# An instruction planner with a readiness slack, a shorter landing margin, early multiply-adds on GpSimd, and row loads cut nine to eight

## The chip, the cores and the metric

The kernel runs on one core of a Trainium2 chip. The time is device microseconds (us) of one execution. A kernel is given by the median of several executions, and two kernels are compared by ratios, which are explained at the result.

## The reference

Two strided convolutions with gelu, a projection, a joint tensor `tanh(fe + ge)` and an output projection; the kernel computes the output and the seven gradients of it.

```python
B, T, D, K, U = 2, 16000, 256, 3, 8           # all bf16
def _fwd_reference(x, w1, w2, g, w_f, w_g, w_o):
    # h = gelu(conv3(x, w1))[:, ::2]           T -> T/2
    # f = gelu(conv3(h, w2))[:, ::2]           T/2 -> T/4 = 4000
    fe = jnp.einsum("btd,de->bte", f, w_f)
    ge = jnp.einsum("bud,de->bue", g, w_g)
    j = jnp.tanh(fe[:, :, None, :] + ge[:, None, :, :])
    return jnp.einsum("btud,dv->btuv", j, w_o)

def reference(x, w1, w2, g, w_f, w_g, w_o, grad_out):
    _out, _vjp = jax.vjp(_fwd_reference, x, w1, w2, g, w_f, w_g, w_o)
    return (_out, *_vjp(grad_out))
```

## The kernel before

The 4,000 output rows of each batch are worked in chunks, 18 in all. The kernel does not write its instructions in a fixed order. Every operation is recorded with the engines that may do it and a modelled cost; a planner then walks through modelled time and hands out the operations. Its key for an operation is the latest start that still meets the modelled end, so a small key is urgent.

```python
class Flow:
    WAKE = {"PE": 45.0, "ACT": 25.0, "DVE": 25.0, "POOL": 280.0, "SP": 60.0}
    MARGIN = 6500.0                              # ns added to a load before its consumers may be placed
    # ...
            for e, lst in avail.items():         # each engine, its operations with all inputs planned
                t, wake, cand = T[e], self.WAKE[e], None
                for o in lst:
                    s = o.ready + wake           # earliest modelled start
                    # ... (DMA lanes, free buffers)
                    k = (max(s, t), o.key, o, e) # first that which can start first, then the urgent one
                    if cand is None or k < cand:
                        cand = k
    # ...
                o.done = ring[e] + 2000.0 + o.margin     # when the planner takes a load to have landed
```

The derivative of gelu is a polynomial on bf16 tiles. Its three one-input steps, here called the multiply-adds, run on VectorE:

```python
    def conv_gelu(W, taps, h_buf, h_ap, g_buf, g_ap, news):
        # ... per half: matmuls -> ps; ScalarE Square -> g_sq, Gelu -> HT or FT; VectorE (g_sq+1)*ps -> g_s
        op("ACT", c_act(N), lambda e: nc.scalar.activation(out=s[:, :, :W], in_=s[:, :, :W], func=ACT.Tanh, scale=c), ...)
        op("DVE", c_dve(N, 0.25), lambda e: nc.vector.tensor_scalar(
            out=sq[:, :, :W], in0=sq[:, :, :W], scalar1=3.0 * c, scalar2=c, op0=ALU.mult, op1=ALU.add), ...)
        op("DVE", c_dve(N, 0.5), lambda e: nc.vector.tensor_tensor(
            out=sq[:, :, :W], in0=sq[:, :, :W], in1=h_ap(None), op=ALU.mult), ...)
        op("DVE", c_dve(N, 0.25), lambda e: nc.vector.tensor_scalar(
            out=sq[:, :, :W], in0=sq[:, :, :W], scalar1=-0.5, scalar2=None, op0=ALU.add), ...)
        op("DVE", c_dve(N, 0.25), lambda e: nc.vector.tensor_scalar(
            out=s[:, :, :W], in0=s[:, :, :W], scalar1=-1.0, scalar2=1.0, op0=ALU.mult, op1=ALU.add), ...)
        op("DVE", c_dve(N, 0.5), lambda e: nc.vector.tensor_tensor(
            out=g_ap(), in0=s[:, :, :W], in1=sq[:, :, :W], op=ALU.mult), ...)
```

Names that the profile uses: FE is the projection of the chunk, copied out of PSUM and transposed by TensorE (`psb<-ident,FE`); JT and JR are the tanh of the joint tensor in two layouts; GWO is the gradient of `w_o`, whose matmuls read JR; OUT and GX are the outputs; X are the rows of `x` for the gradient of `w1`, two overlapping loads of nine rows each for a chunk.

## Time and profile before

| | before |
|---|---|
| median of 3 runs | 807.73 us (807.53 to 807.94) |
| span of the profiled run | 803.7 us |
| columns of all 6,124 matmuls with the small cost of each | about 761 us |
| TensorE / VectorE / ScalarE / GpSimd busy | 97 / 95 / 88 / 11% |

How to read it: three engines are nearly full, so the averages tell little, and the stages must be looked at one by one. The prediction below shows the lines that do so.

### The profile page before, as it was taken

The page shows a single profiled execution, that of the slowest core. Times are in us where ns is not written, and L with a number is a line of the kernel's source. Part 1 is how long each engine was busy: PE and PEld are TensorE (multiplying, and loading weights), DVE is VectorE, ACT ScalarE, POOL GpSimd, SP SyncE. Part 2 cuts the span into 40 slices and gives each one's busy share as a digit, 9 for nine tenths or more (in the row PEclk, how much of TensorE's full clock was granted, in tenths as well). Part 3 has the DMA queues.
Part 4 walks back from the last instruction along what each step waited for, and adds up shares of the span by engine and source line. Part 5 has one row for each costly group of instructions (what it writes and reads, how often), then busy time and mean ns, then how long its engine had stood idle before and what let it go on. Part 6 is the DMA issues. An engine that isn't in the chain of part 4 may idle for free.

```text
span 803.7 us, 16871 instructions
## 1 busy us (share of the span) xinstructions
PE 776.6 (97%) x6124; PEld 574.1 (71%) x6124; DVE 761.3 (95%) x1743; ACT 705.9 (88%) x1138; POOL 87.6 (11%) x256
## 2 busy tenths in 40 slices
PE   8799999999999999999999999999999999999996
PEld 6566667676776867787777667676776867788885
DVE  5989999999999999998989999999999999999894
ACT  6999999998898999997889999998898999997482
POOL 1001110200101010010011100000102000011121
PEclk9989999999999999999999999999999999999999
DMA  7999999999999999999999999999999999999995
GB/s 199 221 219 226 242 228 217 240 244 252 209 277 220 248 257 188 251 214 240 219 230 174 259 252 242 245 228 268 208 261 216 254 256 234 241 232 221 212 216 138
DMA packets 403360, 184.81 MB, mean 230 GB/s; under 512 B 326310, under 2 KB 394956, under 8 KB 403276
## 3 DMA queue, kind: packets, MB, share of 16 engines
q1 hardware_dynamic: 400764, 182.53, 102.8%
q10 hardware_dynamic: 2384, 1.18, 0.5%
q8 instruction: 48, 0.79, 0.4%
q14 instruction: 36, 0.29, 0.1%
q0 software_dynamic: 128, 0.03, 0.0%
HBM read 52.48 MB, written 50.34 MB: 128 GB/s over the span
## 4 chain that ended last, share of the span: by engine, by line
PE 48%; DVE 28%; ACT 19%; issue 3%; DMA 1%; SPq 0%; DVEq 0%; ACTq 0%
PE ps L412 40%; PE GWO L412 7%; DVE NGZ L855 5%; ACT JT L788 5%; DVE ZS L863 5%; ACT JSQ L845 4%; DVE g_s L603 3%; DVE JR L801 2%; ACT g_sq L599 2%; ACT JR L808 2%; DVE ACC L912 2%; ACT HT L601 2%; ACT OUT_SB L423 2%; DVE g_sq L614 1%; DVE GH L971 1%
## 5 line engine op out<-in xcount | busy, mean ns | idle before, releaser
L788 ACT ACTIVATE JT<-FE,GE 128x512 bf16<-128x512 bf16 (+2 forms) x288 | 183.1, 676 | 7.9 <-PE ps L412 6.9
L412 PE MATMUL ps<-GOT,WT 128*128 128x512 bf16 (+3 forms) x640 | 152.5, 333 | 2.6 <-DMA GOT<-GO_R 2.2
L412 PE MATMUL ps<-WO,JT 128*128 128x256 bf16 x1024 | 151.7, 272 | 2.1 <-DVE GH L981 1.7
L855 DVE SCALAR_TENSOR_TENSOR NGZ<-JSQ,ps 128x512 f32<-128x512 bf16 (+2 forms) x252 | 151.5, 605 | 0.0
L808 ACT ACTIVATE JR<-JR 128x1024 bf16<-128x1024 bf16 x128 | 136.4, 1071 | 9.3 <-DVE JR L801 9.2
L845 ACT ACTIVATE JSQ<-JT 128x1024 bf16<-128x1024 bf16 (+2 forms) x128 | 126.2, 986 | 15.8 <-DVE NGZ L855 14.7
L412 PE MATMUL GWO<-GO_R,JR 128*128 128x256 bf16 x1024 | 133.2, 274 | 2.0 <-ACT JR L808 2.0
L412 PEld LDWEIGHTS <-JT 128*128 128x128 bf16 x1024 | 99.0, 98 | 49.0 <-issue 4.6
L863 DVE TENSOR_TENSOR ZS<-ZS,NGZ 128x512 f32<-128x512 f32 (+2 forms) x216 | 131.1, 612 | 0.0
L423 ACT CAST OUT_SB<-ps 128x512 bf16<-128x512 f32 x192 | 110.5, 596 | 22.7 <-PE ps L412 22.6
L412 PEld LDWEIGHTS <-JR 128*128 128x128 bf16 x1028 | 99.6, 98 | 24.8 <-ACT JR L808 4.4
L412 PEld LDWEIGHTS <-WT 128*128 128x128 bf16 x1000 | 88.5, 98 | 39.2 <-issue 4.4
L412 PEld LDWEIGHTS <-W 128*128 128x128 bf16 x720 | 65.9, 98 | 55.0 <-issue 2.3
L412 PE MATMUL ps<-WT,GH 128*128 128x256 bf16 x732 | 97.1, 273 | 0.7 <-DVE NGZ L855 0.7
L412 PE MATMUL ps<-XC,W 128*128 128x512 bf16 (+4 forms) x432 | 93.0, 343 | 1.1 <-DMA XC<-in_x_dram 1.1
L412 PE MATMUL ps<-GHR,X 128*128 128x256 bf16 x768 | 90.5, 273 | 0.0
L801 DVE TENSOR_TENSOR JR<-FER,GEB 128x1024 bf16<-128x1024 bf16 x128 | 87.2, 686 | 0.1
L412 PEld LDWEIGHTS <-X 128*128 128x128 bf16 x768 | 74.9, 98 | 9.7
L412 PEld LDWEIGHTS <-GH 128*128 128x128 bf16 x732 | 71.2, 98 | 12.3 <-issue 1.7
L603 DVE SCALAR_TENSOR_TENSOR g_s<-g_sq,ps 128x512 bf16<-128x512 bf16 (+2 forms) x108 | 65.7, 610 | 12.0 <-ACT HT L601 9.0
L912 DVE TENSOR_TENSOR ACC<-ACC,ps 128x512 f32<-128x512 f32 x96 | 64.7, 678 | 8.5 <-PE ps L412 8.2
L599 ACT ACTIVATE g_sq<-ps 128x512 bf16<-128x512 f32 (+2 forms) x108 | 58.5, 545 | 8.4 <-PE ps L412 7.6
(127 smaller groups left out, 1003.4 us busy)
## 6 DMA issues: line engine op xcount, KB each, us to landing
GO_R<-in_grad_out_dram SPq DMA_DIRECT2D x56, 512.0 KB, 5.1
out_dram<-OUT_SB SPq DMA_DIRECT2D x56, 512.0 KB, 4.5
X<-in_x_dram SPq DMA_DIRECT2D x28, 576.0 KB, 6.1
out_dram<-GX_SB SPq DMA_DIRECT2D x28, 512.0 KB, 6.1
GO_R<-in_grad_out_dram SPq DMA_DIRECT2D x8, 256.0 KB, 5.2
out_dram<-OUT_SB SPq DMA_DIRECT2D x8, 256.0 KB, 2.9
GOT<-GO_R SPq DMA_TRANSPOSE x72, 6.5
out_dram<-w_out SPq DMA_DIRECT2D x9, 128.0 KB, 1.9
```

The costliest lines, as they stand in the source:

```text
L412: nc.tensor.matmul(ps_ap, lhsT=lhsT, rhs=rhs, start=start, stop=stop)
L423: nc.scalar.copy(out=dst(), in_=src())
L599: op("ACT", c_act(W, True), lambda e, mt=mt, ps=ps: nc.scalar.activation(out=sq[:, mt, :W], in_=ps[:, :W], func=ACT.Square, scale=GELU_SQR ...
L601: go = op("ACT", c_act(W, True), lambda e, mt=mt, ps=ps: nc.scalar.activation(out=h_ap(mt), in_=ps[:, :W], func=ACT.Gelu_apprx_tanh), r=[p ...
L603: op("DVE", c_dve(W), lambda e, mt=mt, ps=ps: nc.vector.scalar_tensor_tensor(out=s[:, mt, :W], in0=sq[:, mt, :W], scalar=1.0, in1=ps[:, :W ...
L788: op("ACT", c_act(W, ptr=True), lambda e, j=j, mt=mt: nc.scalar.activation(out=JT[:, j, mt, :W], in_=S["FE"][:, mt, :W], func=ACT.Tanh, bi ...
L801: op("DVE", c_dve(n * 2 * D, 0.5), lambda e, lo=lo, n=n, m=m, JR=JR: nc.vector.tensor_tensor(out=JR[:m, lo % 2:lo % 2 + n], in0=S["FER"][: ...
L808: op("ACT", c_act(n * 2 * D), lambda e, lo=lo, n=n, m=m, JR=JR: nc.scalar.activation(out=JR[:m, lo % 2:lo % 2 + n], in_=JR[:m, lo % 2:lo % ...
L845: nc.scalar.activation(out=JSQ[:, :, :W], in_=JT[:, j, :, :W], func=ACT.Square)
L855: op("DVE", c_dve(W) + 6, lambda e, d2=d2, ps=ps, u=u, zap=zap, JSQ=JSQ: nc.vector.scalar_tensor_tensor(out=zap(), in0=JSQ[:, d2, :W], sca ...
L863: op("DVE", c_dve(W), lambda e, d2=d2, dst=dst, NGZ=NGZ: nc.vector.tensor_tensor(out=dst[:, d2, :W], in0=ZS[:, d2, :W], in1=NGZ[:, :W], op ...
L912: op("DVE", c_dve(512), lambda e: nc.vector.tensor_tensor(out=acc_ap().rearrange("p k d -> p (k d)"), in0=acc_ap().rearrange("p k d -> p ( ...
```

## The change

The planner should prefer operations that have been ready for a while (SLACK), so that an engine isn't put right behind its producer and made to stand by a small modelling error. Loads are taken to land 3 us sooner (MARGIN). The multiply-adds of the first three chunks, where VectorE is full, may go to GpSimd, whose cost the planner takes as 130 ns plus 1 ns a column. The second row load takes eight rows, since the ninth was there already.

```diff
-    MARGIN = 6500.0
+    SLACK = {"PE": 500, "ACT": 300, "DVE": 300, "POOL": 0.0, "SP": 0.0}
+    MARGIN = 3500.0
...
-                    k = (max(s, t), o.key, o, e)
+                    k = (max(s + slack, t), o.key, o, e, max(s, t))
...
+        nr = 9 - h
...
-                                             ap=[[4 * nb * D, hi - lo], [1, 9 * D]]),
+                                             ap=[[4 * nb * D, hi - lo], [1, nr * D]]),
...
+        ts = lambda n: (("POOL", "DVE"), (130.0 + n, c_dve(n, 0.25))) if early else ("DVE", c_dve(n, 0.25))
-        op("DVE", c_dve(N, 0.25), lambda e: nc.vector.tensor_scalar(
+        op(*ts(N), lambda e: (nc.gpsimd if e == "POOL" else nc.vector).tensor_scalar(
   (three times; early is g_ < 3)
```

(Cut: the same slack carried through the planner's loop, the row addresses, and the `early` argument in three calls.)

More of the change, by code (lines that the diff above doesn't have):

```diff
@@ L184, in run @@
             for e, lst in avail.items():
-                t, wake, cand = T[e], self.WAKE[e], None
+                t, wake, cand, slack = T[e], self.WAKE[e], None, self.SLACK[e]
                 for o in lst:
@@ L214, in run @@
                 continue
-            s, _, o, e = best
+            _, _, o, e, s = best
             if o.lead:
@@ L529, in load_x9 @@
         for k, (lo, hi) in enumerate(row_parts(r0, P)):
-            dma(LOADQ, lambda lo=lo, hi=hi: X9[:].rearrange("p f d -> p (f d)")[lo:hi],
-                lambda lo=lo, hi=hi: bass.AP(tensor=src.tensor, offset=src.offset + (4 * (c0 + nb * lo) - 3 + 8 * h) * D,
-                                             ap=[[4 * nb * D, hi - lo], [1, 9 * D]]),
-                r=[], w=[(X9, ("m", k))], bytes_=(hi - lo) * 4608, new=new, at=at, hold=hold, cost=550.0)
+            dma(LOADQ, lambda lo=lo, hi=hi: X9[:, 0:nr].rearrange("p f d -> p (f d)")[lo:hi],
+                lambda lo=lo, hi=hi: bass.AP(tensor=src.tensor, offset=src.offset + (4 * (c0 + nb * lo) - 3 + 9 * h) * D,
+                                             ap=[[4 * nb * D, hi - lo], [1, nr * D]]),
+                r=[], w=[(X9, ("m", k))], bytes_=(hi - lo) * 512 * nr, new=new, at=at, hold=hold, cost=550.0)
             new = []
@@ L582, in part, with conv_gelu @@
         return p_
-    def conv_gelu(W, taps, h_buf, h_ap, g_buf, g_ap, news):
+    def conv_gelu(W, taps, h_buf, h_ap, g_buf, g_ap, news, early=False):
         hk = (lambda mt: (h_buf[0], (h_buf[1], mt))) if isinstance(h_buf, tuple) else (lambda mt: (h_buf, mt))
@@ L615, in conv_gelu @@
             out=sq[:, :, :W], in0=sq[:, :, :W], in1=h_ap(None), op=ALU.mult), r=[sq, hk(0), hk(1)], w=[sq], at=late)
-        op("DVE", c_dve(N, 0.25), lambda e: nc.vector.tensor_scalar(
+        op(*ts(N), lambda e: (nc.gpsimd if e == "POOL" else nc.vector).tensor_scalar(
             out=sq[:, :, :W], in0=sq[:, :, :W], scalar1=-0.5, scalar2=None, op0=ALU.add), r=[sq], w=[sq], at=late)
-        op("DVE", c_dve(N, 0.25), lambda e: nc.vector.tensor_scalar(
+        op(*ts(N), lambda e: (nc.gpsimd if e == "POOL" else nc.vector).tensor_scalar(
             out=s[:, :, :W], in0=s[:, :, :W], scalar1=-1.0, scalar2=1.0, op0=ALU.mult, op1=ALU.add),
@@ L684, in stage_a @@
                 for i, c in ((0, 1), (1, 2), (2, 3)) for kt in range(KT)]
-        conv_gelu(W, (taps, S["XCk"] + [W1]), (HT, "o"), both(HTo, P), G1o, lambda: G1o[:, :, P:P + W], [HT, G1o])
+        conv_gelu(W, (taps, S["XCk"] + [W1]), (HT, "o"), both(HTo, P), G1o, lambda: G1o[:, :, P:P + W], [HT, G1o], g_ < 3)
         for nm, T_, k_, keys in (("HTo", HTo, (HT, "os"), [(HT, ("o", 0)), (HT, ("o", 1))]),
@@ L707, in stage_a @@
         taps += [(lambda kt=kt: W1[:, 0, kt], lo, lambda f=f, kt=kt: f(kt)) for lo, f in S["xback"] for kt in range(KT)]
-        conv_gelu(W, (taps, S["XCk"] + [W1, S["XS"]]), (HT, "e"), both(HTe), G1e, lambda: G1e[:, :, 0:W], [G1e])
+        conv_gelu(W, (taps, S["XCk"] + [W1, S["XS"]]), (HT, "e"), both(HTe), G1e, lambda: G1e[:, :, 0:W], [G1e], g_ < 3)
         if Wp > W:
@@ L717, in stage_a @@
                 for i, SRC, lo in ((2, HTo, P), (1, HTe, 0), (0, HTo, r0)) for kt in range(KT)]
-        S["go"] = [conv_gelu(W, (taps, hok + hek + [W2]), FT, both(FT), G2, lambda: G2[:, :, 0:W], [FT, G2])]
+        S["go"] = [conv_gelu(W, (taps, hok + hek + [W2]), FT, both(FT), G2, lambda: G2[:, :, 0:W], [FT, G2], g_ < 3)]
         pad_tail(g_, FT)
@@ L1020, in stage_de @@
             X5 = [load_x9(b, c0, nb_of[g_], h, t0 + dt * 0.2, hold_) for h in range(nb_of[g_] // 2)]
-            xrow = lambda m, bl, f, d2: X5[bl // 2][:m, bl % 2 * 4 + f, d2 * P:(d2 + 1) * P]
+            xrow = lambda m, bl, f, d2: (X5[0][:m, 4 * bl + f, d2 * P:(d2 + 1) * P] if 4 * bl + f < 9 else
+                                         X5[1][:m, 4 * bl + f - 9, d2 * P:(d2 + 1) * P])
         else:
```

## The prediction

> **What bounds the kernel now.** I read the engine totals on the page first, then the groups of TensorE's instructions by form, then the table of windows, TensorE's waits, and the timeline of the worst place.
>
> ```profile
> PE 776.6 (97%) x6124; PEld 574.1 (71%) x6124; DVE 761.3 (95%) x1743; ACT 705.9 (88%) x1138; POOL 87.6 (11%) x256
> PEclk9989999999999999999999999999999999999999
> ```
>
> TensorE is busy 97% of the 803.7 us span, but VectorE (95%) and ScalarE (88%) stand close behind, so the average does not say which one holds the end in a given stage. The clock row has a dip in its third slice. As busy matmuls overlap, I count columns instead: adding count times width over all matmul forms gives 6,124 matmuls with 1,789,040 columns. Back to back, eight 256-column matmuls take 0.87 us in the chain of waits, 0.109 us each, which is 256 columns at 2.4 per ns plus 2.3 ns. So the floor of TensorE is 745.4 us of columns, about 761 us with the small cost per matmul. 803.7 - 761 leaves **about 42 us in which no column streams**. The windows say where:
>
> ```profile
> core 0: us, PE busy (x) PEld busy (x) DVE busy (x) ACT busy (x) POOL busy (x), PEclk, DMA share, GB/s
> 20.00:40.00 20.00, 15.19 (x112) 10.08 (x110) 19.73 (x57) 18.94 (x36) 1.40 (x4) 0.99 1.11 220
> 40.00:45.00 5.00, 3.26 (x19) 2.36 (x20) 5.00 (x15) 4.66 (x6) 0.89 (x2) 0.50 1.04 267
> 45.00:50.00 5.00, 5.00 (x30) 2.91 (x29) 4.00 (x11) 4.77 (x7) 0.00 (x0) 0.86 0.99 241
> 60.00:80.00 20.00, 18.12 (x134) 12.37 (x133) 20.00 (x46) 19.72 (x31) 3.02 (x7) 1.00 1.01 221
> 80.00:100.00 20.00, 19.62 (x137) 12.78 (x135) 20.00 (x43) 20.00 (x33) 2.63 (x6) 1.00 1.09 243
> 100.00:120.00 20.00, 18.45 (x140) 12.87 (x138) 20.00 (x42) 19.92 (x31) 2.14 (x7) 1.00 1.08 226
> 300.00:400.00 100.00, 99.74 (x843) 76.95 (x842) 96.29 (x230) 87.25 (x155) 11.52 (x39) 1.00 1.03 222
> ```
>
> There are two regimes. From 20 to 120 us VectorE and ScalarE are both full and TensorE is not: the elementwise engines bound this stage. From 120 us TensorE is full and they are not. Adding spacings minus columns over the TensorE timeline, I place the 42 us so: about 6 before 20 us (first loads), about 15 from 20 to 120 us, about 14 spread over 120 to 790 us in waits too short to show as idle time, and about 7 after the last matmul at 796.4 us. Only the middle two, 29 us, can be had by this change. The waits that do show:
>
> ```profile
> PE psb L656 <- DVE FE L428: 4.2, 5, 2.0
> PE ps L412 <- DVE NGZ L855: 3.0, 7, 0.6
> PE ps L412 <- DMA GOT<-GO_R: 2.2, 2, 1.2
> PE GWO L412 <- ACT JR L808: 2.0, 3, 1.0
> PE ps L412 <- DVE GH L981: 1.7, 2, 0.9
> ```
>
> The largest is a matmul put right behind its own producer: the transposes of FE wait for the copy of FE out of PSUM. The worst one is at 39 us:
>
> ```profile
> 40.69 1.28 DVE L428 CAST FE<-ps 128x512 bf16<-128x512 f32 x2
> 41.42 0.29 PE L656 MATMUL psb<-ident,FE 128*128 128x128 bf16 x1 [1.95 <-DVE FE L428]
> 43.17 1.91 PE L412 MATMUL GWO<-GO_R,JR 128*128 128x256 bf16 x8
> ```
>
> VectorE runs back to back from 20 us to here, so the copies start 1.3 us after their matmuls are through. TensorE stands, and then the eight matmuls of GWO take 1.91 us where they take 1.03 to 1.05 elsewhere: the clock has been halved (0.50 in the window 40 to 45 us).
>
> [...] a ZS addition beside GpSimd copies took 0.88 us against a median of 0.68. [...] No multiply-add on GpSimd is in this trace; its memsets grow from 540 ns (512 elements) to 1,166 ns (1,280), or 0.82 ns an element, so I estimate about 1.0 us for 1,024.
>
> **The change part by part.** All numbers of instructions come from comparing the instruction orders of the two kernels.
>
> (1) GpSimd for the early multiply-adds. 22 instructions move, 16 of 1,024 columns and 6 of 512. On VectorE they are spaced 0.34 us and about 0.21 us, so 16 x 0.34 + 6 x 0.21 = 6.7 us leave VectorE in the first 85 us, where it is full. [...] a loss of 0.2 to 0.3 us for each of the 22 gives back 4.4 to 6.6 us. Net **-1 us**, and I would not be surprised by zero.
>
> (2) Operations ready for a while first. TensorE's instructions are the same 6,124 in another order. What changes can be read from the order: the matmul time that stands between the FE matmuls and the transposes that need their copy had a median of 1.4 us over the 18 chunks, with 0.87 four times or so and 0.0 in the second chunk; after, it is 1.96, and 1.5 in the second chunk. [...] So nearly all of the FE wait should go: 2.3 us at 39 to 42 us, and about 2.4 us later. [...] 5 us at 0.50 with 3.26 us busy costs 1.6 us, and 5 us at 0.86 costs 0.7, 2.3 us in all. I give the early pair 2.3 + 2.3 = 4.6 us a probability of 0.7: **-3.2 us**. Of the 14 us from 120 us on I give back the 2.4 of FE and about a quarter of the other 11.6, since the same rule should loosen the waits for NGZ, GH and JR: **-5 us**.
>
> (3) The rebalanced elementwise work. The order also moves 19 squarings of 1,024 columns from ScalarE (1.07 us) to VectorE (0.68 us), and 14 GX and 10 OUT evacuations from VectorE (0.68) to ScalarE (0.60). Every one of these goes to the cheaper place, but for the most part after 120 us, where TensorE bounds. I book **-1 us**, for the early stage.
>
> (4) The landing margin falls from 6.5 to 3.5 us, so consumers are placed up to 3 us nearer to their loads. With the model's own 2 us and 1.7 to 2.6 us of transfer it now expects 7.2 to 8.1 us; the landings measured are 6.5 us in the median for GOT, 5.5 for X, 6.2 for XC, but 9.4, 9.6 and 9.0 at the most. So a few loads will be late, by about 1 us; most are met by the queue of matmuls in front. **+1 us**. It also lets buffers be reused earlier, which I do not count.
>
> (5) X rows in nine and eight: 14 loads shrink by 128 x 512 bytes, 0.9 MB of 184.8. No wait for X shows on TensorE, so **0**.
>
> Sum: -1 - 3.2 - 5 - 1 + 1 = -9.2 us on 807.73, so **798.5 us**, 1.1% less.
>
> **The rivals.** First, [...] GpSimd's long instructions hold VectorE up in the one stage where it is the bound. The 0.88 us ZS speaks for it, the halved GpSimd speed beside VectorE too; against it, GpSimd mostly was the one that waited. Then the early stage gains nothing or loses 3 us, and the time is 802 to 806. Second, *a DMA wait takes the place of the margin*: the share of the DMA engines is already 1.0 to 1.1 in every window, and landings of over 9 us occur. If a tenth of the 72 GOT loads and 32 XC loads came 1 us late, that would be 10 us: 806 to 810. Against it: after 45 us no wait of TensorE for a DMA shows at all, so there is slack that the old margin did not need. Third, *more than I count*: if the clock dip goes, the early stage is freed and half of the 14 us of short waits goes too, 4.6 + 3 + 7 + 1 gives about 792, and both stages well solved would pass 2%.
>
> **Range and chances.** I take 790 to 807 for 8 in 10: the lower end is the third rival with a little more, the upper one the first two in part. To be faster by over 2% the time must be under 791.6, 16 of the 29 us: chance 0.12. Slower by over 2% needs 823.9, a reordering gone badly wrong: 0.03. The rest, 0.85, is within 2%.
>
> **What would show it.** Step (2) is right if the wait for FE falls from 4.2 to under 1 us and the granted clock stays over 0.9 from 40 to 50 us; wrong if either stays. Step (1) is right if the moved instructions take 1.0 us or more on GpSimd and VectorE's two-input instructions beside them lengthen; if VectorE's do not lengthen, I undercounted the gain. Step (4) is wrong if TensorE's waits for GOT, X or GHR pass 3 us. From 120 us on TensorE should stay at 99% or more, with the whole gain there about 5 us; if 120 to 790 us shrinks by under 2 us, the prediction fails on step (2).

- The floor: in the traces of before and after, matmuls of 128, 256 and 512 columns follow each other back to back after 56, 109 and 216 ns in the median. That is 2.4 columns per ns, and 2.3 to 2.7 ns for each matmul.
- Step (1): that VectorE loses 0.2 to 0.3 us for each moved operation. The one loss named there is of 0.2 us (ZS, 0.88 for 0.68); the upper end was not shown. The halved GpSimd speed of the first rival is that of the 128x254 copies in before: 0.39 to 0.41 us in 42 of 70 cases, but 0.76, 0.79 and 0.90 us at 21.8, 65.4 and 97.1 us, beside VectorE's JR and G1o (TENSOR_TENSOR).
- Step (2): how much matmul time the FE copy needs was put together from latencies that were not measured. In before, the copy of 512 columns begins 0.41 us after the start of its last matmul where it begins soonest (0.40 to 0.42 us, six times, on ScalarE), takes 0.68 us on VectorE, and the transposes that waited start 0.06 us after its end, 1.15 us in sum. That the clock would stay up without the stand, worth 2.3 us, was assumed. What the half clock costs can be seen: the matmuls in it follow each other after 213 and 427 ns for 256 and 512 columns.

## More of the kernel before

One row is added here, the stage from 20 to 120 us as a whole (columns: window and its length; busy us and instructions of TensorE, its weight loads, VectorE, ScalarE, GpSimd; granted clock; share of DMA engines; GB/s):

```profile
20.00:120.00 100.00, 89.54 (x638) 60.33 (x637) 97.63 (x230) 96.92 (x155) 11.03 (x30) 0.97 1.06 227
```

## The result, and the profile after

| | before | after |
|---|---|---|
| median, 4 runs each, same rounds | 807.63 us (805.54 to 807.94) | 805.7 us (804.54 to 807.0) |
| ratio | | 0.9982, 95% interval 0.9958 to 1.0006 |
| span of the profiled run | 803.7 us | 802.8 us |

Ratios here and below are the mean time of one kernel's fast runs over that of the other's of the same rounds, so not quite the ratio of the medians. The change gave 0.2%, with an interval that includes no gain at all; 798.5 us was predicted.

The page of the changed kernel, its engine totals and its clock row:

```profile
PE 775.1 (97%) x6124; PEld 574.3 (72%) x6124; DVE 762.2 (95%) x1711; ACT 695.5 (87%) x1137; POOL 118.8 (15%) x289
PEclk9999999999999999999999999999999999999999
```

VectorE has 32 instructions fewer and is 0.9 us busier (762.2 against 761.3). GpSimd works 31 us more. The dip in the clock row is gone at this scale. The windows, with the columns named above:

```profile
20.00:40.00 20.00, 13.31 (x101) 9.05 (x99) 18.61 (x50) 18.59 (x36) 13.23 (x9) 1.00 1.03 181
40.00:45.00 5.00, 4.49 (x20) 2.55 (x21) 4.87 (x16) 3.51 (x7) 1.16 (x3) 0.66 1.11 294
45.00:50.00 5.00, 5.00 (x36) 3.00 (x34) 5.00 (x13) 4.56 (x9) 2.78 (x3) 1.00 0.97 233
60.00:80.00 20.00, 17.23 (x126) 11.86 (x124) 20.00 (x40) 18.52 (x28) 9.50 (x12) 1.00 0.99 213
...
300.00:400.00 100.00, 100.00 (x847) 77.43 (x845) 95.96 (x226) 88.40 (x157) 12.80 (x43) 1.00 1.02 228
```

Where GpSimd is busy (13.23 us in 20 to 40, 9.50 in 60 to 80), TensorE does less than before: 13.31 for 15.19, and 17.23 for 18.12. Where GpSimd has none of the moved work, it does a little more: 100.00 for 99.74 in the late window. The waits of TensorE (what waits, for what, total us, times, longest):

```profile
PE GWO L413 <- ACT JR L811: 4.7, 4, 2.2
PE ps L413 <- DVE g_s L605: 3.6, 5, 1.1
PE ps L413 <- DMA GFR<-GF: 2.0, 2, 1.4
PE psb L659 <- DVE FE L429: 2.0, 1, 2.0
PE ps L413 <- DVE NGZ L858: 1.9, 4, 0.8
```

The wait for FE fell from 4.2 to 2.0 us, but the wait of GWO for JR rose from 2.0 to 4.7, and one for g_s came up. The timeline shows the new worst places:

```profile
22.43 0.34 PE L659 MATMUL psb<-ident,FE 128*128 128x128 bf16 x3 [1.95 <-DVE FE L429]
...
30.49 1.05 PE L413 MATMUL GWO<-GO_R,JR 128*128 128x256 bf16 x8 [1.86 <-ACT JR L811]
...
40.51 1.05 PE L413 MATMUL GWO<-GO_R,JR 128*128 128x256 bf16 x8 [2.16 <-ACT JR L811]
41.40 2.55 PE L413 MATMUL ps<-HT,W 128*128 128x512 bf16 x6
```

TensorE stands at 40 us as it did before, 2.16 us for JR in place of 1.95 us for FE, and again a half clock is seen: the six matmuls of HT take 2.55 us where six of the same form took 1.46 us at 36.68. The order of events differs, though. In after the clock falls at 41.6 us, behind the stand, and is back at 45.0. In before it fell at 39.6 us, when the stand for FE had lasted 0.13 us (TensorE's last matmul ended at 39.47), and was back only at 46.4:

```profile
39.40:39.60 0.20, 0.07 (x1) 0.00 (x0) 0.20 (x2) 0.18 (x1) 0.00 (x0) 0.98 1.28 292
39.60:39.80 0.20, 0.00 (x0) 0.00 (x0) 0.20 (x1) 0.00 (x0) 0.00 (x0) 0.50 1.27 288
```

So the prediction misreads this place where it puts the half clock down to the stand for FE: the fall came after smaller waits, of 0.92 us for a load of GOT, 0.36 for NGZ and 0.19 for FT, between 36.4 and 38.7 us. ScalarE's timeline says why JR was late:

```profile
37.06 0.63 ACT L848 ACTIVATE JSQ<-JT 128x512 bf16<-128x512 bf16 x1 [0.99 <-DVE NGZ L858]
37.59 0.57 ACT L424 CAST OUT_SB<-ps 128x512 bf16<-128x512 f32 x1
38.06 1.06 ACT L611 ACTIVATE g_s<-g_s 128x1024 bf16<-128x1024 bf16 x1
39.02 0.50 ACT L791 ACTIVATE JT<-FE,GE 128x256 bf16<-128x256 bf16 x1
39.42 1.04 ACT L811 ACTIVATE JR<-JR 128x1024 bf16<-128x1024 bf16 x1
```

ScalarE waited 0.99 us for VectorE at 36 us, then four operations stood ahead of JR in its order, back to back.

To place gains and losses I count the **time in which no column streams**: a stage's length less the columns of the matmuls in it (columns over 2.4 ns, and 2.5 ns for each matmul, after the 56, 109 and 216 ns measured for 128, 256 and 512 columns). Over the whole run 760.7 us are columns (1,789,040 columns and 6,124 matmuls), so the rest is the span less 760.7. Each row is one profiled execution. In the traces marked * 41 or 43 records of matmuls are missing, all 512 columns wide; their weight loads are all there (6,124), so each is put back at the place of its weight load:

| us without columns | 0 to 20 | 20 to 120 | 120 to 780 | 780 to end | all |
|---|---|---|---|---|---|
| before | 6.0 | 16.1 | 12.4 | 8.5 | 43.0 |
| after | 7.5 | 17.7 | 8.3 | 8.5 | 42.0 |
| a_nopool: after, nothing on GpSimd, planned anew | 7.3 | 14.4 | 7.8 | 8.4 | 37.9 |
| a_vec: after, its order, the 22 back on VectorE | 7.2 | 15.7 | 6.9 | 7.5 | 37.4 |
| a_twoop: after, its order, a faster form on GpSimd | 7.5 | 15.3 | 7.5 | 7.8 | 38.1 |
| b_pool: before, the choice of GpSimd alone | 6.7 | 17.7 | 12.7 | 8.1 | 45.2 |
| b_slack*: before, SLACK alone | 10.6 | 14.2 | 5.7 | 7.6 | 38.1 |
| b_drop*: before, its order, 27 left out | 6.6 | 14.9 | 13.1 | 7.8 | 42.4 |

How fine such a count is can be seen from after, a_vec and a_twoop: they have one order of instructions and differ only before about 85 us, yet from 120 to 780 us they have 8.3, 6.9 and 7.5. So a difference below about 1.5 us tells nothing by itself. Nor is each profile of a median execution: that of a_nopool is of one of its longer ones (800.43 us, median 798.59), that of after of the fastest of its four (804.54 us, median 805.7).

The first two rows hold the answer in outline. From 120 to 780 us the change gained 4.1 us. In the first 20 us it lost 1.5, from 20 to 120 us 1.6, and at the end nothing. (This count puts 16.1 and 12.4 us where the prediction had about 15 and 14. The expectations below quote an earlier count, 11.3 and 4.9 us for the late stage and 25.8 up to 120 us; by this one they are 12.4, 4.1 and 25.2.) The loss at the start begins with ScalarE, of before and of after:

```profile
7.90 0.38 ACT L599 ACTIVATE g_sq<-ps 128x256 bf16<-128x256 f32 x1 [5.20 <-PE ps L412]
```

```profile
10.38 0.37 ACTq L441 DMA_DIRECT2D WO<-in_w_o_dram  x1
10.80 0.38 ACT L601 ACTIVATE g_sq<-ps 128x256 bf16<-128x256 f32 x1 [4.11 <-DMA W<-in_w_dram]
```

In the new order the load of `w_o` stands in ScalarE's queue behind a copy that waits for TensorE, then waits for an earlier load, and goes out at 10.38 us (at 4.51 before). The first activation of a chunk comes behind it, at 10.80 us in place of 7.90.

### The profile page after: what moved, and what is told of

Same layout as the page of the kernel before. It is cut to its first block, busy times and chain, and to the rows that moved or that the text cites. A ratio compares the mean times of both kernels' runs of the same rounds, so it can differ in the third digit from the quotient of the medians.

```text
span 802.8 us, 16870 instructions
## 1 busy us (share of the span) xinstructions
PE 775.1 (97%) x6124; PEld 574.3 (72%) x6124; DVE 762.2 (95%) x1711; ACT 695.5 (87%) x1137; POOL 118.8 (15%) x289
## 4 chain that ended last, share of the span: by engine, by line
PE 71%; DVE 19%; issue 3%; DMA 3%; POOL 1%; ACT 1%; DVEq 0%; POOLq 0%; ACTq 0%
PE ps L413 60%; PE GWO L413 10%; DVE NGZ L858 3%; DVE ZS L866 3%; DVE g_s L605 2%; DVE JR L804 2%; DMA GFR<-GF 2%; DMA W<-in_w_dram 1%; DVE g_sq L617 1%; POOL g_sq L619 1%; DVE OUT_SB L429 1%; DVE GH L974 1%; PE psb L659 1%; DVE JSQ L850 1%; DVE g_s L621 1%
## 5 line engine op out<-in xcount | busy, mean ns | idle before, releaser
L791 ACT ACTIVATE JT<-FE,GE 128x512 bf16<-128x512 bf16 (+2 forms) x288 | 186.8, 710 | 0.4
L858 DVE SCALAR_TENSOR_TENSOR NGZ<-JSQ,ps 128x512 f32<-128x512 bf16 (+2 forms) x252 | 153.9, 614 | 0.3 <-PE ps L413 0.2
L424 ACT CAST OUT_SB<-ps 128x512 bf16<-128x512 f32 x202 | 124.1, 620 | 23.9 <-PE ps L413 22.2
L811 ACT ACTIVATE JR<-JR 128x1024 bf16<-128x1024 bf16 x128 | 140.1, 1103 | 5.4 <-DVE JR L804 5.2
L866 DVE TENSOR_TENSOR ZS<-ZS,NGZ 128x512 f32<-128x512 f32 (+2 forms) x216 | 135.2, 630 | 0.4
L848 ACT ACTIVATE JSQ<-JT 128x1024 bf16<-128x1024 bf16 (+2 forms) x109 | 108.9, 999 | 20.2 <-DVE NGZ L858 19.3
L413 PE MATMUL ps<-WT,GH 128*128 128x256 bf16 x732 | 100.0, 274 | 0.8 <-DVE NGZ L858 0.5
L804 DVE TENSOR_TENSOR JR<-FER,GEB 128x1024 bf16<-128x1024 bf16 x128 | 89.7, 703 | 0.6 <-PE GWO L413 0.6
L413 PEld LDWEIGHTS <-X 128*128 128x128 bf16 x768 | 75.0, 98 | 10.6 <-issue 0.2
L601 ACT ACTIVATE g_sq<-ps 128x512 bf16<-128x512 f32 (+2 forms) x108 | 60.9, 564 | 18.2 <-PE ps L413 12.5
```

What stands on the lines that cost most here:

```text
L413: nc.tensor.matmul(ps_ap, lhsT=lhsT, rhs=rhs, start=start, stop=stop)
L424: nc.scalar.copy(out=dst(), in_=src())
L601: op("ACT", c_act(W, True), lambda e, mt=mt, ps=ps: nc.scalar.activation(out=sq[:, mt, :W], in_=ps[:, :W], func=ACT.Square, scale=GELU_SQR ...
L791: op("ACT", c_act(W, ptr=True), lambda e, j=j, mt=mt: nc.scalar.activation(out=JT[:, j, mt, :W], in_=S["FE"][:, mt, :W], func=ACT.Tanh, bi ...
L804: op("DVE", c_dve(n * 2 * D, 0.5), lambda e, lo=lo, n=n, m=m, JR=JR: nc.vector.tensor_tensor(out=JR[:m, lo % 2:lo % 2 + n], in0=S["FER"][: ...
L811: op("ACT", c_act(n * 2 * D), lambda e, lo=lo, n=n, m=m, JR=JR: nc.scalar.activation(out=JR[:m, lo % 2:lo % 2 + n], in_=JR[:m, lo % 2:lo % ...
```

## The experiments

My theory after the result: SLACK earned what was predicted late in the run, and the multiply-adds on GpSimd lost it again from 20 to 120 us. Rivals: the landing margin or the new order as such lost it; or SLACK earned nothing and the stage's other differences are accidents of a new order. Twelve kernels were run with five rounds each. All but the last compute the right result.

**a_vec: the order of after, the moved operations issued on VectorE.**

```diff
-        op(*ts(N), lambda e: (nc.gpsimd if e == "POOL" else nc.vector).tensor_scalar(
+        op(*ts(N), lambda e: nc.vector.tensor_scalar(
```

> The changed kernel with its own order on every engine, but the 22 multiply-adds that it puts on GpSimd are issued to VectorE at the same places of the order. Theory G (GpSimd's work costs the early stage: [...]): the moved work costs VectorE 6.7 us again [...] so this is faster than the changed kernel by 2 to 4 us (801.5 to 803.5 us), and TensorE's time without columns up to 120 us falls from 25.8 to about 22 to 24 us. Theory O (the new order itself is worse at the start, first of all the load of w_o that stands in ScalarE's queue before its first activations): no gain or a loss, 805 to 808 us, and 25 to 28 us without columns up to 120 us.

Measured: 800.93 us (798.84 to 803.38) against 805.4, ratio 0.9946 (0.9926 to 0.9966). With nothing else changed, taking the 22 operations back makes the kernel 0.36% or about 2.9 us faster than after (0.9982), as theory G had it, though the two intervals meet by a hair (0.9966 and 0.9958). It also gives the size of what VectorE loses beside GpSimd. The page's totals here:

```profile
PE 775.7 (97%) x6124; PEld 574.4 (72%) x6124; DVE 762.0 (95%) x1733; ACT 695.7 (87%) x1137; POOL 87.5 (11%) x267
```

VectorE is busy 762.0 us with 1,733 instructions here and 762.2 us with 1,711 in after. By the prediction's spacings the 22 should have taken 6.7 us away, so the rest of its work grew by about 6.9 us, 0.31 us for each operation moved. As the order is the same, VectorE's instructions can also be paired one by one: those that run beside a moved operation are 6.6 us longer in after, in sum (12 of 80 by over 0.1 us, the longest by 0.84), all others of the first 95 us 0.4 us.

**b_gps: the order of before, all 27 early multiply-adds on GpSimd.**

```diff
-        op("DVE", c_dve(N, 0.25), lambda e: nc.vector.tensor_scalar(
+        op("DVE", c_dve(N, 0.25), lambda e: (nc.gpsimd if early else nc.vector).tensor_scalar(
```

> The kernel before with its own order on every engine, but all 27 multiply-adds of the first three chunks are issued to GpSimd at the same places. Theory G: slower than before by 3 us or more (over 810.5 us), VectorE's two-input instructions beside them take up to 1.2 us. Theory O: GpSimd is as good as VectorE here, within 1.5 us of before (806 to 809 us).

Measured: 821.52 us (819.55 to 823.34), ratio 1.0197 (1.0178 to 1.0215). All 27 moved, without the planner's choice, cost 2%. Two facts of the trace of after say why GpSimd is a bad place. The first is the duration of the moved operations (line, form, count, busy us, mean ns, idle time before them):

```profile
L619 POOL TENSOR_SCALAR g_sq<-g_sq 128x1024 bf16<-128x1024 bf16 x4 | 11.6, 2893 | 7.1 <-DVE g_sq L617 7.1
...
L614 POOL TENSOR_SCALAR g_sq<-g_sq 128x1024 bf16<-128x1024 bf16 x6 | 7.3, 1210 | 11.8 <-DVE g_s L605 11.8
L621 POOL TENSOR_SCALAR g_s<-g_s 128x1024 bf16<-128x1024 bf16 x6 | 7.3, 1209 | 5.2 <-ACT g_s L611 5.2
```

L614 and L621 multiply and add; L619 only adds -0.5, one operation less, and takes 2.4 times as long, in b_gps too (2,813 ns). The planner took all three at 1.15 us. The second is what VectorE does beside them, in the timeline of after:

```profile
24.33 1.35 POOL L614 TENSOR_SCALAR g_sq<-g_sq 128x1024 bf16<-128x1024 bf16 x1 [1.54 <-DVE g_s L605]
24.69 1.26 DVE L850 TENSOR_TENSOR JSQ<-JT 128x512 bf16<-128x512 bf16 x1
```

The squaring JSQ has two SBUF inputs. It takes 0.41 to 0.42 us elsewhere in this stretch; here it takes 1.26 us, and is through 0.27 us after the GpSimd operation that it started beside.

**a_nopool: after, planned anew with the early multiply-adds for VectorE only.**

```diff
-        ts = lambda n: (("POOL", "DVE"), (130.0 + n, c_dve(n, 0.25))) if early else ("DVE", c_dve(n, 0.25))
+        ts = lambda n: (("POOL", "DVE"), (130.0 + n, c_dve(n, 0.25))) if False else ("DVE", c_dve(n, 0.25))
```

> The changed kernel without the choice of GpSimd for the multiply-adds, planned anew: the other three parts are kept. Theory G: 801 to 803.5 us, the gain of the stage after 120 us (4.9 us less time without columns) is kept and the loss of the early one mostly goes. Theory O: 805 to 808 us, since ScalarE's queue still has the late load of w_o ahead of its first activations and the early order is still that of the preference for ready operations.

Measured: 798.59 us (796.1 to 801.48), ratio 0.9916 (0.9895 to 0.9936), which is where the prediction was, and better than either theory had it. Its interval does not meet that of after. In the table it gains 3.3 us of 4.1 on after between 20 and 120 us. Its windows:

```profile
40.00:45.00 5.00, 5.00 (x31) 2.79 (x29) 4.97 (x16) 4.22 (x9) 0.31 (x2) 1.00 1.10 269
45.00:50.00 5.00, 4.03 (x31) 2.39 (x30) 5.00 (x14) 5.00 (x10) 0.00 (x0) 1.00 1.07 226
```

Here the clock does stay up (1.00, 1.00). Yet TensorE's wait for JR is still 4.2 us, and the stage from 20 to 120 us gained only 1.7 us on before.

**a_twoop: after, the lone addition written as a multiply by 1.0 and an addition.**

```diff
-            ... scalar1=-0.5, scalar2=None, op0=ALU.add), r=[sq], w=[sq], at=late)
+            ... scalar1=1.0, scalar2=-0.5, op0=ALU.mult, op1=ALU.add), r=[sq], w=[sq], at=late)
```

> The changed kernel, same order on every engine, but the subtraction of a half is written as a multiply by 1 and an add, the two-operation form that the other multiply-adds have. If the 2.8 us that it takes on GpSimd, against 1.06 us in the median for the two-operation form, come from the one-operation form, it falls to about 1.1 us for 1,024 elements; [...]. Theory G: 1 to 2 us faster than the changed kernel (803.5 to 805 us). Theory O: no change, within 0.7 us of it.

Measured: 801.92 us (800.18 to 804.3), ratio 0.9959 (0.9941 to 0.9977). The same group as above:

```profile
L619 POOL TENSOR_SCALAR g_sq<-g_sq 128x1024 bf16<-128x1024 bf16 x4 | 4.7, 1167 | 7.7 <-DVE g_sq L617 7.7
```

The same values in the same order, by a two-operation form: 1,167 ns for 2,893. So the slowness is that of the form on GpSimd, as VectorE's work has the same order beside both. About 0.2% of the time seems to come back, but the interval meets that of after, so the size is unsure. VectorE's loss stays: paired with a_vec as above, VectorE's instructions beside the moved ones are still 6.0 us longer. The time remains above a_nopool.

**b_slack: before with SLACK alone.**

```diff
+    SLACK = {"PE": 500, "ACT": 300, "DVE": 300, "POOL": 0.0, "SP": 0.0}
-                    k = (max(s, t), o.key, o, e)
+                    k = (max(s + slack, t), o.key, o, e, max(s, t))
```

> The kernel before with the preference for operations ready for a while, and nothing else. If this part is what shortens the stage after 120 us (4.9 us less time without columns in the changed kernel, 120 to 780 us), this kernel has most of that: at most 8 us there instead of 11.3, and 800 to 803 us. If the shorter landing margin did it, 11 us stay there and the time is 804 to 807 us.

Measured: 799.87 us (797.66 to 800.71) against 805.82, ratio 0.9915 (0.9898 to 0.9933). This one part carries the whole gain of a_nopool. Its early stage is no tidier for it:

```profile
40.00:45.00 5.00, 2.31 (x13) 1.16 (x11) 5.00 (x17) 4.53 (x9) 1.71 (x6) 0.86 1.22 233
...
PE GWO L413 <- ACT JR L809: 5.3, 3, 2.7
```

Between 40 and 45 us TensorE works 2.31 us, less than before, and the wait for JR is 5.3 us, the longest 2.7: it has the place of the wait for FE (1.8 us now). The table says where the gain is: 12.4 to 5.7 us without columns from 120 to 780 us, under the 8 us that were asked for if SLACK is what shortens this stage. From 20 to 120 us it gains 1.9, and in the first 20 us it loses 4.6.

**b_margin: before with the margin of 3.5 us alone.**

```diff
-    MARGIN = 6500.0
+    MARGIN = 3500.0
```

> The kernel before with the landing margin at 3.5 us, and nothing else. My prediction booked 1 us of loss by late loads: then 805.5 to 808 us, with waits of TensorE for DMAs of 1 to 4 us after 60 us. If the margin is what gained, 800 to 803 us. If it matters to nothing, within 1 us of before.

Measured: 805.61 us (804.61 to 806.87), ratio 0.9993 (0.9975 to 1.0011). The margin does nothing to the time that can be seen. TensorE's largest waits for a DMA are 1.6 us for NFR, 1.1 for XC and 1.1 for GHR.

**b_rows: before with the rows in nine and eight alone** (the diff is that of the change's `load_x9` and `xrow`).

> The kernel before with x rows in nine and eight, and nothing else. Booked as 0: within 1 us of before. If the DMA engines, whose busy share is 1.0 to 1.1, are a bound, 0.9 MB of 184.8 less should show as 2 to 4 us.

Measured: 804.42 us (802.92 to 807.16), ratio 0.998 (0.996 to 1.0). Small, and at the edge of what five rounds tell; as it changes the plan, I do not put it down to the bytes saved.

**c_nopool_x9: a_nopool, and the first small row load held back like the others.** The planner keeps loads in eight lanes; the six-row load at the very start takes one of them, and the load of `w_o` had to wait for one.

```diff
-                r=[], w=[(X9, "b")], bytes_=3072, at=at, cost=550.0)
+                r=[], w=[(X9, "b")], bytes_=3072, at=at, hold=hold, cost=550.0)
```

> The changed kernel without GpSimd for the multiply-adds, and with the first tiny load of an x row held until after the first gelu, so that the load of w_o goes out in front of ScalarE's work and its first activation starts at about 8 us instead of 10.8. If the late w_o costs the early stage what it delays (up to 2.5 us), this is 796 to 798 us against 798.6 without it; if the start is hidden by the backlog that follows, no change, within 1 us of it.

Measured: 797.23 us (795.76 to 797.77, four fast runs) against 805.82, ratio 0.9884 (0.9866 to 0.9903). The load of `w_o` goes out at 5.70 us and the first activation starts at 8.21 us, 2.25 sooner than in a_nopool (10.46). The interval meets that of a_nopool (from 0.9895 on), so this pair alone does not settle that the early load is worth anything.

**b_pool: before with the planned choice of GpSimd alone** (the change's `ts` and `early`, SLACK zero, MARGIN 6500, rows as before).

> The kernel before with the choice of GpSimd for the early multiply-adds, planned with it, and nothing else. All 27 on GpSimd in an unchanged order cost 2%. Theory G: planned, it costs about the 0.7% by which the changed kernel is behind the one without this part, so 809 to 813 us. If the loss in the changed kernel came from this part only together with the preference for ready operations: within 1.5 us of before.

Measured: 808.56 us (807.84 to 809.93) against 806.32, ratio 1.0034 (1.002 to 1.0048). By itself, planned, the choice costs 0.34%. In the table it loses 1.6 us from 20 to 120 us, and less than a count can tell elsewhere. Its clock is not the cause: it stays at full speed until 802 us (0.998 in the mean of the run, 0.994 in before), without the dip that before has.

**c_twoop_x9: after, with the two-operation form and the small load held back.** (Both diffs are shown above.)

> The changed kernel with all its parts, with the two-operation form of the subtraction (1.17 us on GpSimd instead of 2.89) and with the early load of w_o. If GpSimd's help is worth something once its slow form is gone, this beats the same kernel without GpSimd (797.2 us): 793 to 796 us. [...]

(The sentence cut above put 796.5 to 799 us on the case that VectorE loses what the moved work saves.)

Measured: 797.76 us (796.45 to 799.57), ratio 0.9896 (0.9879 to 0.9913). Against a_twoop (0.9941 and up) holding the small load back is worth 0.6%, and these intervals do not meet. As it also makes a new plan, I can't say how much of that is the earlier load. Against c_nopool_x9 the use of GpSimd, in its fast form, is worth nothing: 0.9896 and 0.9884. The planner put 22 operations on GpSimd here too, so in this plan the moved work costs no 5 us either.

**d_slack2: c_nopool_x9 with twice the slack.**

```diff
-    SLACK = {"PE": 500, "ACT": 300, "DVE": 300, "POOL": 0.0, "SP": 0.0}
+    SLACK = {"PE": 1000, "ACT": 600, "DVE": 600, "POOL": 0.0, "SP": 0.0}
```

> The kernel without GpSimd's multiply-adds and with the early load of w_o, with the preference doubled (1,000 ns for TensorE, 600 for ScalarE and VectorE). If the gain comes from waits that are shorter than what the preference bridges, a dose of twice the size gains 1 to 2 us more after 120 us (795 to 796 us); if 500 and 300 ns already bridge them, no more there and some loss at the start (797 to 800 us).

Measured: 796.93 us (795.93 to 799.23), ratio 0.9888 (0.9871 to 0.9905). Twice the slack gives the same.

**b_drop: before in its order, the 27 early multiply-adds left out; the result is wrong.**

```diff
-        op("DVE", c_dve(N, 0.25), lambda e: nc.vector.tensor_scalar(
+        op("DVE", c_dve(N, 0.25), lambda e: None if early else nc.vector.tensor_scalar(
```

> The kernel before in its own order, with the 27 multiply-adds of the gelu' polynomial of the first three row chunks left out altogether; the results are wrong on purpose. It is the upper bound of what any offload of them to GpSimd could give. If VectorE's load sets the time of the early stage, as step 1 of my prediction took it, 27 operations of about 0.31 us (8.4 us of VectorE's time) come off and the time falls by 3 to 8 us, to 798 to 803 us. If the early stage is held by the order, by ScalarE and by the first loads, the time stays within 1.5 us of the kernel before.

Measured: 804.13 us (803.24 to 805.48) against 805.88, ratio 0.9975 (0.9957 to 0.9993). A perfect offload, with nothing in return, gives 2 us in this order (0.6 to 3.5 by the interval). It bounds what an offload gives in this order alone, and not, as the expectation says, that of any offload: a planner that knows of it could make more of it. The 2 us lie between the two expectations and nearer the second. Its stage from 20 to 120 us:

```profile
20.00:120.00 100.00, 90.67 (x643) 61.38 (x647) 93.15 (x214) 97.53 (x156) 8.79 (x30) 0.97 1.07 227
```

VectorE is down from 97.63 to 93.15 us, and TensorE is up by only 1.13 us (89.54 to 90.67; five matmuls are missing from the record, so it is a little more: by columns the stage gains 1.2). ScalarE is as full as before: 97.53.

The fastest correct runs, c_nopool_x9, d_slack2 and c_twoop_x9, beat both kernels, by 1.0 to 1.2% against before.

## Why the prediction was wrong

It said 9.2 us less; the ratio says about 1.5 us less (0.18% of 806). The steps that failed are (1) and the early half of (2), both for the stage from 20 to 120 us: it was to gain 5.2 us and lost 1.6. By its own steps:

**Step (1), GpSimd for the early multiply-adds, booked at -1 us: this step failed.** a_nopool and after differ by 0.9916 to 0.9982, which is 0.66% or about 5 us, on the wrong side; alone, planned, it is 0.34%, about 2.7 us. Two terms were mis-sized, and a third was about right.
- *The worth of VectorE's time.* The step took each microsecond off VectorE in this stage as one off the end. b_drop took 6.4 us of VectorE's busy time off (761.3 to 754.9) and the end moved by 2: ScalarE was full beside it.
- *The duration on GpSimd.* About 1.0 us was estimated for all; it is 1.2 us for the multiply-and-add forms and 2.9 for the lone addition. The estimate came from memsets and could not see the form. VectorE stands 2.4 us for GpSimd's results in after, 0.2 in a_twoop and not at all in a_vec. a_twoop and after put the form at some 0.2% of the time, with overlapping intervals.
- *What VectorE loses beside GpSimd* was booked at 0.2 to 0.3 us for each operation. It is 0.31 by the spacings, 0.30 by the paired instructions, and 0.25 if b_drop is the measure (6.4 us for 27 is 5.2 us for 22, and 0.2 us came on top). Either way VectorE gained nothing, which the step had said would not surprise.

The first rival had the right range, 802 to 806, and the right reason for a gain of nothing: VectorE was held up by as much (6.9 us) as it was relieved of. That alone does not make the loss: it is there in a_twoop (6.0 us), which is faster than after, and c_twoop_x9 moves as many operations at no cost that can be told. Beyond it, the moved steps stand in a chain of dependent operations, each of them now 1.2 to 2.9 us for 0.34. That this delay is the rest of the 5 us is argued, not shown. a_vec against a_nopool, 0.9946 and 0.9916, suggests that part of the cost is in the plan made for GpSimd: the same operations on VectorE in that plan are slower than in a plan without it, though these intervals meet by a hair.

**Step (2), early half, booked at -3.2 us: did not come.** The step held that nearly all of the FE wait should go, and that without the stand at 39 us the clock need not fall (an assumption). Its own signs were a wait for FE under 1 us and a clock over 0.9 from 40 to 50 us: they are 2.0 us and 0.66 (40 to 45 us). In after the wait for FE fell by 2.2 us, while that for JR grew by 2.7, and the stand of 2.16 us at 40 us came before a clock of 0.66. The link to the clock was misread as well, since in before it fell at 39.6 us, ahead of nearly all of that stand. Without GpSimd (a_nopool) the clock is 1.00, and the stage gains 1.7 us, half of what was booked; the start, up to 20 us, gives back 1.3. The step counted the waits that could vanish and not those that take their place where two elementwise engines are full.

**Step (2), late half, booked at -5 us: right.** The table shows 12.4 to 8.3 us without columns, -4.1, from one profile each; a_nopool has -4.6. b_slack shows that SLACK alone makes this gain: -6.7 us in this stage, 0.85% of the time in all. The same step of "what would show it" asked for over 2 us here, and got it.

**Step (3), the rebalanced elementwise work, booked at -1 us:** not separated from the plan by any run; what it could give in the early stage is within the terms above.

**Step (4), the margin, booked at +1 us:** 0.9993 with an interval of 0.0018 to either side, -2.0 to +0.9 us, so the +1 is just outside and the second rival did not happen.

**Step (5), the rows, booked at 0:** 0.998 with an interval that ends at 1.0; right within what can be told.

**What had no step** was the beginning: up to 20 us after loses 1.5 us, by the count, as the load of `w_o` and the first activation move back by 5.9 and 2.9 us. b_slack shows the same late load (10.31 us) and loses 4.6 us there, so it comes with SLACK. Predicted and measured thus differ, stage by stage in one profiled run each: 20 to 120 us, -5.2 booked and +1.6 found; 0 to 20, 0 and +1.5; the end, 0 and 0; 120 to 780, -4 with the margin and -4.1. But for rounding, the found ones sum to -0.9 us, the difference of the two spans.

The parts do not add up either: SLACK -0.85%, margin -0.07, rows -0.20 and GpSimd +0.34 make -0.78%, and the whole has -0.18%. The choice of GpSimd cost about twice as much together with SLACK as alone (0.66 and 0.34%, with intervals that overlap). Why is open: each part makes a new plan of all instructions, and no run holds the plan fixed while it changes the slack.

## What to carry to other kernels

Before moving work off a full engine, leave it out altogether in one run, wrong result and all: here VectorE was relieved of 6.4 us and the time fell by 2, with a second engine as full beside it. (That bounds the offload in the order as it is, not in a new plan.) Measure an operation on the engine it is to go to, in its very form, and what its neighbours pay. A planner's rule that loosens tight hand-overs paid here in the long stage where one engine bounds (6.7 us alone); in the stage where several are full it mostly moved the wait to the next hand-over (1.9 us).

## What the traces show of the forms, the neighbours and the clock

- The two-operation `tensor_scalar` on 128x1024 bf16 took GpSimd 1.17 to 1.21 us in the mean (a_twoop, after) and 1.04 at the least. The one-operation addition took 2.89 us for the same tile (in after; 1.63 for 512 columns, against 0.61 to 0.81), and 1.17 when written with a multiply by 1.0 (a_twoop).
- A squaring of 0.42 us took VectorE 1.26 us beside such an operation (after). Over the stage, 22 GpSimd operations cost VectorE about 6.9 us here, as much as they relieved it of.
- The clock was at half from 39.59 to 46.42 us in before (6.83 us), and from 41.61 to 45.03 us in after (3.41 us). TensorE did not stand all the while before: in the 3.41 us before these falls columns streamed for 1.16 and 1.09 us. What brings the fall about is not shown. The busy share of another window does not foretell it: from 40 to 45 us, 4.49 us busy went with a granted clock of 0.66 (after), 2.31 us busy with 0.86 (b_slack).
